# Two units of 128, 160 or 192 tokens with stationary weights, in place of an expert's last two tiles

## The chip, the core and the metric

The kernel runs on one core of one Trainium2 chip. Its time is the device time of one execution in microseconds; the time before is the median of three runs, 766.85 us (766.51 to 767.8). The core has five engines with instruction streams of their own: TensorE (PE in the profile; PEld is its loading of weights), VectorE (DVE), ScalarE (ACT), GpSimd (POOL) and SyncE (SP). Each works through its stream in order and waits on semaphores for the others. SP issues the loads of weights here, and POOL issues gathers and scatters of single rows.

## The reference, cut to what matters

The first half is block-sparse attention over 4 x 8 heads of 768 tokens. The change leaves its arithmetic alone. Its result is laid out as 3072 rows of 512 numbers, and each row goes through one of eight experts:

```python
N, D, E, F = (3072, 512, 8, 1024)
logits = x @ w_gate
expert_idx = np.argmax(logits, axis=1)
...                                   # gate_w: the softmax weight of the expert that was chosen
for e in range(E):
    lo, hi = (boundaries[e], boundaries[e + 1])
    h = np.maximum(x_sorted[lo:hi] @ w1[e], 0.0)      # layer 1: 512 -> 1024
    y_sorted[lo:hi] = h @ w2[e]                       # layer 2: 1024 -> 512
y = y_sorted[inv_perm]
return (gate_w[:, None] * y).astype(np.float32)
```

Everything is float32. How many rows an expert gets is known on the chip only, during the run. For the inputs of this case the reference gives

| | expert 0 | 1 | 2 | 3 | 4 | 5 | 6 | 7 |
|---|---|---|---|---|---|---|---|---|
| rows in all | 431 | 32 | 256 | 32 | 256 | 160 | 593 | 1312 |
| rows left after the first five tiles | 175 | 32 | 256 | 32 | 128 | 32 | 465 | 1312 |
| tiles of 128 that these need | 2 | 1 | 2 | 1 | 1 | 1 | 4 | 11 |

The first five tiles (`KA = 5`, phase A) are laid out while the last quarter of the attention still runs, from the first three quarters of the rows. The rest (phase B) is laid out once all rows are there: 23 tiles, so 28 in all.

## The kernel before: what the change touches

A tile is 128 rows of one expert. Its rows are gathered, turned so that features lie on the partitions, and taken through the two layers. In layer 1 the weights are stationary and 128 tokens move past them, in layer 2 the tokens are stationary and 512 columns of weights move.

```python
def layer1(i, *between):
    hT = st[i]["hT"] = xp.tile([P, FB, P], F32, name="hT")
    for g in range(2):
        hp = upper["ps_h"].tile([P, FB // 2, P], F32, name="hp")     # two PSUM banks in this pool
        for m in range(FB // 2):
            fb = g * (FB // 2) + m
            for c in range(DB):
                nc.tensor.matmul(hp[:, m, :], lhsT=st[i]["w1"][:, c, fb * P : (fb + 1) * P],
                                 rhs=st[i]["xT"][:, c, :], start=(c == 0), stop=(c == DB - 1))
        if g == 0 and i >= KA:
            nc.vector.tensor_relu(hT[:, : FB // 2, :], hp[:])
        else:
            nc.scalar.activation(hT[:, g * (FB // 2) : (g + 1) * (FB // 2), :], hp[:], AF.Relu)
        if g == 0:
            for do in between:
                do()

def layer2(i, group):
    zp = upper["ps_z"].tile([P, DM], F32, name="zp")
    for fb in range(FB):
        nc.tensor.matmul(zp[:], lhsT=st[i]["hT"][:, fb, :], rhs=st[i]["w2"][:, fb, :],
                         start=(fb == 0), stop=(fb == FB - 1))
    ...   # ScalarE scales by the gate weight, GpSimd scatters the 128 rows to the output
```

The loop over tiles; `fetch` loads 2 MB of weights into one of two buffers of its layer, `turn_x` turns the rows (on VectorE from the seventh tile on). Two points matter below: the layout of phase B (`layout_b`, a chain of small VectorE operations) runs beside tiles 1 and 2, and `tokens("B", ...)`, 24 small matmuls that need the last result of that chain, stands in TensorE's stream ahead of the second layer of tile 1.

```python
for i in range(NT):                       # NT = 24 tiles in any case, the rest in one arm of a switch
    if i == 0:
        ranks("B", TA, NT)
    gather(i + 3)
    if i + 1 < NT:
        layer1(i + 1, lambda: turn_x(i + 2))
        fetch(i + 3, 1)
    if i == 0:
        count("B")
        layout_b()
    if i == 1:
        tokens("B", NT, NB_)
    layer2(i, "rows_out")
    fetch(i + 2, 2)
    ...
for arm in tc.Switch(nc.values_load(rt["arm"][0:1, 0:1], min_val=0, max_val=REDO), REDO + 1):
    ...                                   # arm 4 here: tiles 24 to 27
```

The end of the chain of `layout_b`:

```python
og = [left > 128 * t for each t]; nt = sum(og); up = running sum of nt   # five operations
tile_experts("B", up, NB_)            # xeB: the expert of each tile, read by the loads of weights
...                                   # offsets of each expert's rows, the slot of each row
one_hots("B", sl, NT, NB_)            # sl -> row and tile number -> ocB, tkB, and orB in 4 pieces of 6
```

(The first line is shortened to words; the operations are in the whole kernel.)

## Time and profile before

| | |
|---|---|
| time, median of three | 766.85 us |
| span of the profiled execution | 765.7 us |
| TensorE busy | 749.5 us, 98% of the span |
| VectorE / ScalarE / GpSimd busy | 415.8 / 270.2 / 67.2 us |
| attention, first matmul of the first tile | up to about 357 us |
| tiles, from there to the last matmul | about 357 to 755 us |
| bytes moved by DMA | 157.57 MB, mean 206 GB/s; 300 to 360 GB/s in most slices of the tile stage |

How to read the profile: its second part cuts the span into 40 slices and gives each engine's busy share in tenths; its fourth part follows the chain of work that ended last back from the end, and says for each piece which engine held it; its fifth part groups instructions by the source line, with the number of instructions, the busy time, the mean duration of one, and the idle time just ahead of them with what ended it. An engine that is busy 98% of the span and holds 86% of the chain is the one whose work sets the time. Matmuls overlap, so their durations are longer than their spacing: the spacing is what counts, and it is read from the chain. A float32 matmul of the source appears as two instructions in the trace: 32 matmuls of a tile's layer 1 as 64, and 8 of layer 2 as 16.

### The profile page before, as it was taken

How to read it: one execution, taken by the hardware profiler on the slowest of the kernel's cores; microseconds unless marked ns; L12 is line 12 of the kernel's file. 1: busy time of each engine (PE TensorE's matmuls, PEld its weight loads, DVE VectorE, ACT ScalarE, POOL GpSimd, SP SyncE). 2: the span in 40 equal slices, each digit the busy share in tenths (PEclk: the TensorE clock that was granted, in tenths of full speed). 3: DMA queues.
4: the chain of work that ended last, by engine and by line, in shares of the span. 5: the costliest groups of instructions: out<-in, count | busy, mean ns of one | idle time of the engine just before them, and what ended most of it. 6: DMA issues, size and time to landing. Idle time of an engine off the chain costs nothing.

```text
span 765.7 us, 13053 instructions
## 1 busy us (share of the span) xinstructions
PE 749.5 (98%) x5134; PEld 475.8 (62%) x5134; DVE 415.8 (54%) x834; ACT 270.2 (35%) x425; POOL 67.2 (9%) x98
## 2 busy tenths in 40 slices
PE   7999999999999999999999999999999999999994
PEld 4555555555555555556777686786776776866682
DVE  4678777777778779997530235533434425323400
ACT  4666676667666675665111000100100100001000
POOL 4000000000000000002011121111111211211010
PEclk8999999999999999999999999999999999999998
DMA  8322333233322331842789989899899899899940
GB/s 187 83 60 48 82 84 85 63 83 84 85 56 51 83 84 44 319 165 78 244 308 333 344 311 348 320 329 346 320 329 362 314 344 345 320 346 339 355 147 6
DMA packets 119362, 157.57 MB, mean 206 GB/s; under 512 B 56499, under 2 KB 72947, under 8 KB 119284
## 3 DMA queue, kind: packets, MB, share of 16 engines
q1 hardware_dynamic: 112672, 142.42, 55.8%
q0 software_dynamic: 4480, 13.75, 4.6%
q8 instruction: 43, 0.70, 0.4%
q10 hardware_dynamic: 2132, 0.41, 0.3%
q14 instruction: 35, 0.29, 0.1%
HBM read 143.79 MB, written 13.73 MB: 206 GB/s over the span
## 4 chain that ended last, share of the span: by engine, by line
PE 86%; DMA 7%; issue 5%; another core or an unknown queue 0%; ACTq 0%; POOL 0%; ACT 0%; DVE 0%; POOLq 0%
PE hp L661 21%; PE zp L676 19%; PE s L216 17%; PE op L237 16%; DMA out_dram<-zo,sB 6%; PE s L219 4%; PE sp L250 3%; PE xr L270 3%; PE tp L199 2%; DMA q_sb<-in_q_dram 1%; PE tpg L650 0%; POOL xg L620 0%; ACT qT L201 0%; ACTq L117 0%
## 5 line engine op out<-in xcount | busy, mean ns | idle before, releaser
L661 PEld LDWEIGHTS hp<-xgT,w 128*128 128x128 f32 x1792 | 204.7, 192 | 12.6 <-issue 8.6
L661 PE MATMUL hp<-xgT,w 128*128 128x128 f32 x1792 | 205.6, 275 | 0.0
L676 PE MATMUL zp<-w,hT 128*128 128x512 f32 x448 | 196.9, 593 | 0.0
L642 DVE STREAM_TRANSPOSE xgT<-xg 32x128 f32<-32x128 f32 x352 | 106.5, 303 | 110.0 <-DMA xg<-x_rows,gB 94.0
L216 PE MATMUL s<-qT,kT 64*128 64x384 f32 x768 | 159.2, 493 | 0.9 <-ACT qT L201 0.9
L221 ACT ACTIVATE e<-s 128x768 f32<-128x768 f32 x192 | 152.4, 812 | 7.0 <-PE s L219 5.2
L676 PEld LDWEIGHTS zp<-w,hT 128*128 128x128 f32 x448 | 83.0, 190 | 94.2 <-issue 94.2
L227 DVE TENSOR_TENSOR esum<-esum,e 128x768 f32<-128x768 f32 x128 | 122.7, 958 | 14.6 <-ACT e L221 1.1
L237 PE MATMUL op<-e,v_sb 128*64 128x384 f32 x768 | 129.3, 486 | 0.0
L237 PEld LDWEIGHTS op<-e,v_sb 128*64 128x64 f32 x768 | 55.1, 137 | 68.8 <-issue 68.8
L216 PEld LDWEIGHTS s<-qT,kT 64*128 64x128 f32 x768 | 67.1, 190 | 38.4 <-issue 33.5
L257 DVE RECIPROCAL r<-ss 128x128 f32<-128x128 f32 x96 | 82.2, 912 | 1.3 <-ACT ss L252 1.3
L668 ACT ACTIVATE hT<-hp 128x512 f32<-128x512 f32 x33 | 19.7, 597 | 177.4 <-PE hp L661 174.4
L681 ACT ACTIVATE zo<-zp,xg 128x512 f32<-128x512 f32 x28 | 19.2, 687 | 176.7 <-PE zp L676 176.7
L666 DVE TENSOR_SCALAR hT<-hp 128x512 f32<-128x512 f32 x23 | 15.9, 692 | 101.4 <-issue 57.9
L227 DVE TENSOR_TENSOR esum<-e 128x768 f32<-128x768 f32 x32 | 30.6, 957 | 63.2 <-ACT e L221 63.2
L219 PE MATMUL s<-pen,oh 64*128 64x384 bf16 x384 | 63.2, 326 | 0.0
L242 ACT COPY oT<-op 128x384 f32<-128x384 f32 x32 | 15.3, 479 | 106.2 <-PE op L237 106.2
L682 POOL DMA_INDIRECT out_dram<-zo,sB x23 | 23.3, 1013 | 259.7 <-ACT zo L681 259.7
L219 PEld LDWEIGHTS <-oh 64*128 64x128 bf16 x384 | 18.9, 95 | 25.8 <-issue 0.9
L270 PEld LDWEIGHTS xr<-mix,oT 128*64 128x64 f32 (+1 forms) x372 | 24.0, 139 | 10.7 <-issue 10.7
L250 PE MATMUL sp<-esum,ones 128*64 128x384 f32 x128 | 27.7, 512 | 0.0
(174 smaller groups left out, 260.1 us busy)
## 6 DMA issues: line engine op xcount, KB each, us to landing
w<-in_moe_w_dram SPq DMA_DIRECT2D x56, 2048.0 KB
k_sb<-in_k_dram SPq DMA_DIRECT2D x32, 192.0 KB
v_sb<-in_v_dram SPq DMA_DIRECT2D x16, 384.0 KB
x_rows<-xb SPq DMA_DIRECT2D x16, 384.0 KB
q_sb<-in_q_dram SPq DMA_DIRECT2D x30, 192.0 KB
sums<-ss SPq DMA_DIRECT2D x32, 3.0 KB
q_sb<-in_q_dram ACTq DMA_DIRECT2D x2, 192.0 KB
xg<-x_rows,gB POOLq DMA_INDIRECT x23, 7.5
```

Of the source, the lines that this page charges most:

```text
L216: nc.tensor.matmul(s[:, hh, :CW], lhsT=kT[r, c * P : (c + 1) * P], rhs=qT[r, cols], start=True, stop=False)
L219: nc.tensor.matmul(s[:, hh, :CW], lhsT=oh[r, c, :], rhs=pen[r, cols], start=False, stop=True)
L221: nc.scalar.activation(e[:], s[:, :, :CW], AF.Exp, scale=scale)
L227: nc.vector.tensor_add(t[:], es[(n, half, 0)][:] if c == 1 else t[:], e[:])
L237: nc.tensor.matmul(op[hh * D : (hh + 1) * D, :], lhsT=v_sb[:, hh, c, :], rhs=e[:, hh, :], start=(c == 0), stop=(c == NCH - 1),)
L250: nc.tensor.matmul(sp[hh * D : (hh + 1) * D, :], lhsT=ones[:], rhs=esum[:, hh, :], start=True, stop=True)
L257: nc.vector.reciprocal(r[:, m * P : (m + 1) * P], ss[:, m * P : (m + 1) * P])
L270: nc.tensor.matmul(xr[j * M_ : (j + 1) * M_, m, :], lhsT=oT[:, m * P + j * M_ : m * P + (j + 1) * M_], rhs=mix[:, pr, :], start=True, stop ...
L642: nc.vector.transpose(xT[d, :, t], xg[t, :DM].rearrange("p (c q) -> p c q", c=DB)[:, :, d])
L661: nc.tensor.matmul(hp[:, m, :], lhsT=st[i]["w1"][:, c, fb * P : (fb + 1) * P], rhs=st[i]["xT"][:, c, :], start=(c == 0), stop=(c == DB - 1),)
L676: nc.tensor.matmul(zp[:], lhsT=st[i]["hT"][:, fb, :], rhs=st[i]["w2"][:, fb, :], start=(fb == 0), stop=(fb == FB - 1),)
L682: ins = nc.gpsimd.indirect_dma_start(out=out[:, :], out_offset=bass.IndirectOffsetOnAxis(ap=of("s", i, P), axis=0), in_=zo[:], in_offset=N ...
```

## The change: what it does and what it is for

The aim is to spare TensorE the work on rows that aren't there: a tile of 128 costs the same with 47 rows in it as with 128. A unit takes up to 192 tokens of one expert through both layers at once. Up to two experts get one, first those whose last tile has at most 64 rows and who have at least two tiles left (it takes the place of the last two tiles), then, if there are fewer than two such, any with a tile left (128 tokens, in place of one tile). In a unit the weights are stationary in both layers, so that the tokens move and their number is free: 128, 160 or 192. The output of layer 2 comes out turned and is turned back by TensorE. The kind is read from memory, and TensorE and ScalarE jump to one of three versions of the code.

With the counts above, expert 0 (175 rows left, 47 in its last tile) gets the first unit with 192 columns, and expert 7 (1312 left, 32 in its last tile) the second with 160. 23 tiles of phase B become 19, and two units; 21 tiles stand outside the last switch in place of 24, and its arm has 3 in place of 4.

```diff
+    AT = (10, 13)                       # the units stand ahead of layer 2 of tiles 10 and 13
+    KU = len(AT)
+    NS = KA - -(N - KA * P - KU * MW) // P                   # 21
+    NTB = NC - KA
+    NB_ = NTB + 2 * KU                                       # 26 -> 30 columns of the slot table
...
+    ea = mpool.tile([P, 8, NCH * P], F32, name="ea")         # the attention's e, 8 slots as before;
-        e = work.tile([P, 2, CW], F32, name="e", bufs=8)     # the units use its memory later
+        e = e_slot(n, half, c)
...
-            oT = work.tile([P, CW], F32, name="oT", bufs=4)
+            oT = work.tile([P, CW], F32, name="oT", bufs=3)
-        r = work.tile([P, CW], F32, name="r")
+        r = work.tile([P, CW], F32, name="r", bufs=1)
... # in summed(), for each of its two calls in layout_b:
+            nc.vector.tensor_tensor(ge[:], slot[:], wide(units[0]), op=ALU.is_ge)
+            nc.vector.tensor_tensor(ge[:], ge[:], wide(units[1]), op=ALU.mult)
+            nc.vector.tensor_tensor(slot[:], slot[:], ge[:], op=ALU.add)
... # in layout_b, ahead of tile_experts: 19 operations on 128 x 8
+        nc.vector.tensor_scalar_mul(last[:], nt[:], -float(P))
+        nc.vector.tensor_single_scalar(v_[:], nt[:], 2.0, op=ALU.is_ge)
+        nc.vector.scalar_tensor_tensor(u[:], in0=last[:], scalar=float(QR), in1=v_[:], op0=ALU.is_le, op1=ALU.mult)
+        nc.vector.tensor_tensor_scan(us[:], u[:], rt["zero"][:], 0.0, op0=ALU.add, op1=ALU.add)
+        ... 
+        nc.vector.tensor_sub(nt[:], nt[:], in_u[:])
... # and behind it: 8 for the units' experts and kinds (xeU), 3 for until and jump
+    def layers_u(u, width, banks):
+        for g in range(4):
+            hp = banks[g].rearrange("p (m t) -> p m t", m=2)
+            for m in range(2):
+                fb = 2 * g + m
+                for c in range(DB):
+                    nc.tensor.matmul(hp[:, m, :width], lhsT=st_u[u]["w1"][:, c, fb * P : (fb + 1) * P],
+                                     rhs=xT_u[:, c, :width], start=(c == 0), stop=(c == DB - 1))
+            nc.scalar.activation(hT_u[:, 2 * g : 2 * g + 2, :width], hp[:, :, :width], AF.Relu)
+        for d in range(DB):
+            zp = banks[d][:, :width]
+            for fb in range(FB):
+                nc.tensor.matmul(zp, lhsT=st_u[u]["w2"][:, fb, d * P : (d + 1) * P], rhs=hT_u[:, fb, :width],
+                                 start=(fb == 0), stop=(fb == FB - 1))
+            nc.scalar.copy(zT_u[:, d, :width], zp)
+        for j in range(2 if width > P else 1):
+            ...                          # 4 transposes each on TensorE, scaled by ScalarE into zo_u
... # in the loop over tiles:
+        if i + 3 in AT:
+            gather_u(AT.index(i + 3))    # two gathers of 128 rows by GpSimd
+        if i + 2 in AT:
+            turn_u()                     # 24 transposes of 32 x 128 on VectorE
+        if i in AT:
+            continue
+        if i + 1 in AT:
+            u = AT.index(i + 1)
+            ...                          # six banks: both of ps_h, both of ps_m, both of ps_z
+            layer2_pe(i, zps[0])
+            fetch_after(i, 2)
+            for more in tc.Switch(index, 3):          # on TensorE and ScalarE
+                weigh(i, zos[0], zps[0])
+                layers_u(u, P + more * QR // 2, banks)
+                layer2_pe(i + 1, banks[1])
+                weigh(i + 1, zos[1], banks[1])
+            fetch_after(("unit", u), 1)
+            fetch_after(("unit", u), 2)
+            fetch_after(i + 1, 2)
+            put(of("s", i, P), zos[0][:], "rows_out")
+            leave_u(u, "rows_out")                    # two scatters
+            put(of("s", i + 1, P), zos[1][:], "rows_out")
+            continue
         layer2(i, "rows_out")
```

With this TensorE's order around the first unit is: layer 1 of tile 10, layer 2 of tile 9, the unit, layer 2 of tile 10, layer 1 of tiles 11 and 12, layer 2 of tile 11. The two buffers of each layer's weights take turns in that order.

## The prediction

> **What bounds the kernel now.** I read the page's shares of busy time first, then the chain of work that ended last, with its pieces in order of time, then the timelines of TensorE and VectorE around 375 to 395 us, where the layout of phase B runs.

> ```profile
> PE 749.5 (98%) x5134; PEld 475.8 (62%) x5134; DVE 415.8 (54%) x834; ACT 270.2 (35%) x425; POOL 67.2 (9%) x98
> ...
> PE 86%; DMA 7%; issue 5%; another core or an unknown queue 0%; ACTq 0%; POOL 0%; ACT 0%; DVE 0%; POOLq 0%
> ```

> TensorE has no idle time to speak of, and holds the chain. The chain in order of time gives a tile's price:

> ```profile
> 425.81 7.14 PE hp L661 x64
> 432.95 6.87 PE zp L676 x16
> 439.82 7.14 PE hp L661 x64
> 446.96 6.87 PE zp L676 x16
> ```

> Each piece begins where the last one ends. A tile costs 7.14 + 6.87 = 14.01 us, as full as it may be. Per instruction that is 7.14/64 = 0.1116 us for 128 moving columns and 6.87/16 = 0.4294 us for 512. The line through both is 5.7 ns and 0.8275 ns a column.

> VectorE's timeline (start, duration) at the layout, and TensorE's at the same time:

> ```profile
> 374.39 0.17 DVE L454 COPY cnB<-lay 128x16 f32<-128x16 f32 x1 [3.83 <-PE lay L452]
> ...
> 376.98 0.17 DVE L475 CAST xeB<-xfB 1x26 int32<-1x26 f32 x1
> ...
> 383.09 3.56 DVE L564 TENSOR_TENSOR orB<-iota_r,rcB 128x768 bf16<-128x768 f32 x4
> ```
> ```profile
> 388.74 0.79 PE L593 MATMUL lay<-tkB,orB 128*128 128x52 bf16 x24
> 389.36 7.11 PE L676 MATMUL zp<-w,hT 128*128 128x512 f32 x16
> ```

> orB is done at 386.65, and TensorE comes to it at 388.74: 2.1 us of slack in a chain of 12.3 us.

> The queries on the switch and on the gathers:

> ```profile
> L761 PEldq TENSOR_LOAD <-arm x1: 487/487/487, 691.1 to 691.1; - x1
> L761 PEldq BRANCH_PREFETCH_HINT  x1: 50/50/50, 695.4 to 695.4; - x1
> ```
> ```profile
> DMA to landing us min/median/max: 7.0/7.7/8.1
> ```

> The first shows the switch of the kernel before: TensorE's sequencer reads its index at 691.1 us and is in the arm at 695.4, but its matmuls run without a gap until the arm's first at 698.76. The second is the time of a row gather in the tile stage (560 to 620 us); in the attention, with less traffic, the same gather took a median of 3.6 us.

> [...] at 691.1 all 32 loads and matmuls of a layer 2 that begins at 691.9 were handed over. [...] Here that took TensorE about 3.3 us, and ScalarE and VectorE about 6 us (their branches at 699.8 and 683.1, their arms at 706.1 and 689.1). [...] this trace shows two instructions for each float32 matmul of the source, each at 0.8275 ns a column[...]; I use its spacing. [...] in this trace one of 8 columns lasts 0.17 us and its dependent successor starts 0.20 us after it.

> **The change part by part.** The attention's order and waits are the same on TensorE, ScalarE and VectorE when I set the two programs side by side; smaller rings for oT and r and the fixed slots of e add no wait there. So I count only the tile stage.

> *Removed:* two tiles of expert 0 and two of expert 7, 4 x 14.01 = 56.04 us of TensorE.

> *Added, the units' matmuls:* 32 per layer in the source, 64 in the trace, 128 for both layers. At 192 columns 5.7 + 192 x 0.8275 = 164.6 ns, at 160 columns 138.1 ns: 21.07 and 17.68 us, 38.75 us together.

> *Added, turning the result back:* eight transposes per unit. Four took 0.44 us in this trace (361.86 to 362.30), so 0.9 us, ahead of which TensorE waits for ScalarE's last copy out of PSUM (some 0.33 us by the sizes of its other copies, and two semaphores) with half of the transposes beside it: 0.35 us. Both units: 2.5 us. ReLUs between the layers cost nothing: the last is needed by the 13th matmul of the second layer, 1.7 us or more after the first layer ends, and lasts about 0.5 us.

> *Added, the switches:* at the entry 6.9 us of layer 2 are queued, and the branch needs 3.3, in the worst case the 6 us of the others. The same at the exit, behind layer 2 of the next tile. Nothing.

> *Added, the longer layout:* VectorE's stream gains 19 operations of 8 columns ahead of xeB. By their waits 13 of them follow what they need (0.20 us or a little less), 6 don't (0.09 us, as 376.98 to 377.07 shows): 3.2 us. Eight for the units' kinds: 1.3 us. Three for until and jump: 0.4. Three of 128x144 (0.345 us from start to start) and three of 128x48 (0.245): 1.75. ocB and both tkB grow from 26 to 30 columns: 0.36. Sum 7.0 us, all ahead of orB. orB ends at 393.65 in place of 386.65; with the semaphore and the last six small matmuls (0.3 us) layer 2 of tile 1 starts at about 393.95 in place of 389.52: **4.4 us** of TensorE standing still. The loads of weights don't suffer: xeB is ready at about 380.3, and the load that comes next waits for a buffer until 381.35.

> *Added, behind each unit:* the unit takes the pool's two PSUM banks out of step. In the built program both halves of layer 1 of tile 11, and of tile 14, lie in the same bank, so the second half has to wait for VectorE's ReLU of the first. Undisturbed that is a semaphore (0.25 us), 0.69 us and another semaphore: 1.1 us. For tile 14 I take that. For tile 11 VectorE's stream has six of the second unit's transposes ahead of that ReLU, and they wait for the second unit's gather. It is issued behind two scatters of the first unit, about 26.5 us after the unit starts (22.3 us of unit, 0.7 us of scaling twice on ScalarE, 1.3 us per scatter). TensorE is through with the first half at 22.3 + 6.9 + 3.6 = 32.8. With 3.6 us of gather the rows land at 30.4 and nothing is lost beyond 1.1 us; with 7.7 us at 34.5, and then transposes (2.0), ReLU and semaphore make it 37.4, 4.6 us. Loads of weights are sparser beside a unit, so I take 2.2 us. Both: **3.3 us**.

> *Moved off the path:* two experts' weights fewer, 8.4 MB. Loads were issued when a buffer came free (SP's own waits name hp and zp for 143 and 138 us) and TensorE never waited for one, so they give nothing back. In the program after, the loads for tiles 11 and 12 are released inside the switch, by each layer of the unit.

> Sum: -56.04 + 38.75 + 2.5 + 4.4 + 3.3 = -7.1 us; 766.85 - 7.1 = 759.8 us. I predict **759.6 us**.

> **The rivals.** (1) The layout's wait is hidden, because TensorE can be behind by then, or because operations of 8 columns overlap more than I count: then 755 us. Against it: TensorE's stream is fixed there and had 2.1 us of slack only. (2) The weights pile up: during a unit of some 20 us only two loads are asked for, and behind it layers of 7 us follow each other. If the load for tile 12 were released only at the switch's end, it would come about when it is needed, and the next ones late: 3 to 6 us per unit, 766 to 770 us. Against it: it is released by the unit's own first layer, some 18 us ahead of its use. (3) The jumps aren't hidden [...]: up to 3 us at each of four branches, 765 us or more. Against it: the old switch cost nothing under the same load. (4) The gather of the second unit is as slow as in the trace's tile stage: 762 us. (5) With narrow moving tiles the loading of weights sets the pace: PEld takes 192 ns each, but at 128 columns they already follow at 111.6 ns, and at 160 and 192 there is more room.

> **Range and chances.** The gain of the units alone (14.8 us) is below 2% (15.3 us), so faster by over 2% would need all waits gone and more. Slower than 782 us would need the rivals all together. The range is set by the layout's wait (3.5 to 5.5), the waits behind the units (2.2 to 6) and jumps (0 to 3): 756.0 to 763.0. Chances: faster 0.02, within 2% 0.96, slower 0.02.

> **What would show each step.** In the profile after: 24 tiles of 14.01 us in the chain (1536 and 384 instructions of the two layers); 128 instructions of unit matmuls in about 21.1 us for the first unit and 17.7 for the second; a hole in TensorE of about 4.4 us ahead of the 24 matmuls of tokens, ended by VectorE's orB; a hole of 1 to 4.6 us inside layer 1 of tile 11 and of about 1.1 us inside that of tile 14, both ended by VectorE's ReLU; no hole at the switches' entries and exits; no wait of TensorE for weights. I am wrong if the attention's part isn't the same to a microsecond, if TensorE waits for a load of weights, or if a jump shows as a hole.

## The result and the profile after

The kernel after takes 763.04 us (median; 761.92 to 763.64), the kernel before 766.85: a ratio of 0.9947, with an interval of 0.9929 to 0.9964. The change brings 3.8 us (by the interval 2.8 to 5.4) where 7.3 were predicted; the median lies at the upper edge of the range that was given (756.0 to 763.0).

The page of the kernel after: the shares of busy time, the clock granted to TensorE in 40 slices, and the chain of work that ended last.

```profile
PE 738.1 (97%) x5086; PEld 477.4 (63%) x5086; DVE 413.3 (54%) x850; ACT 273.9 (36%) x437; POOL 67.1 (9%) x100
...
PEclk8999999999999999999999999999999999999997
...
PE 48%; issue 37%; DMA 7%; POOL 4%; DVE 2%; another core or an unknown queue 0%; ACTq 0%; POOLq 0%; ACT 0%
```

TensorE has 11.4 us less to do by its busy time (749.5 to 738.1), and the span shrinks by 5.1 (765.7 to 760.6). The chain is not the one that the prediction looked for: this time it runs from the last scatter back along GpSimd's own order ("issue" is time in which GpSimd waited for nothing that is on record), and GpSimd is busy 9% of the span. Such a chain names no bound; the idle time of TensorE does. TensorE's waits (engine and line, what ended them, us in all, times, the longest), first before and then after:

```profile
PE bm L162 <- DVE allow L155: 2.6, 1, 2.6
...
```
```profile
PE lay L658 <- DVE orB L629: 3.4, 4, 1.8
PE hp L748 <- DVE hT L753: 3.0, 2, 2.1
PE bm L175 <- DVE allow L168: 2.6, 1, 2.6
...
```

The waits left out are 1.4 us or less and the same ones in both. Two waits are new, both of those that the prediction named: the layout's and the one behind the units. None is a wait for weights. The first new wait in the timelines of the kernel after (start, duration, and in brackets the idle time before it), VectorE and then TensorE:

```profile
389.60 3.56 DVE L629 TENSOR_TENSOR orB<-iota_r,rcB 128x768 bf16<-128x768 f32 x4
```
```profile
390.61 0.34 PE L658 MATMUL lay<-tkB,orB 128*128 128x60 bf16 x6 [1.81 <-DVE orB L629]
391.52 0.34 PE L658 MATMUL lay<-tkB,orB 128*128 128x60 bf16 x6 [0.57 <-DVE orB L629]
392.35 0.34 PE L658 MATMUL lay<-tkB,orB 128*128 128x60 bf16 x6 [0.48 <-DVE orB L629]
393.22 0.34 PE L658 MATMUL lay<-tkB,orB 128*128 128x60 bf16 x6 [0.53 <-DVE orB L629]
393.40 8.81 PE L762 MATMUL zp<-w,hT 128*128 128x512 f32 x16
```

orB is done at 393.16, and layer 2 of tile 1 starts at 393.40 in place of 389.36; the tile stage began 0.1 us earlier, so that the wait is 4.13 us. (Holes below are taken in this way, from where the next instruction would have started at full pace. The bracket counts from the modelled end of the one before and is up to 0.2 us less.) But look at the last line: the same 16 instructions took 7.03 us elsewhere, here 8.81. The granted clock goes with it. This view cuts the time into stretches: busy time of each engine (with the number of instructions), then the granted clock, the DMA engines' share and GB/s.

```profile
390.60:394.20 3.60, 2.01 (x26) 1.33 (x27) 3.09 (x7) 0.00 (x0) 0.00 (x0) 1.00 0.99 348
394.20:397.60 3.40, 3.40 (x5) 1.35 (x4) 2.63 (x9) 0.00 (x0) 1.90 (x2) 0.50 0.92 325
397.60:401.00 3.40, 3.40 (x9) 1.52 (x8) 1.21 (x5) 0.00 (x0) 0.00 (x0) 1.00 0.28 88
...
547.80:551.20 3.40, 1.26 (x12) 1.13 (x11) 3.24 (x11) 0.00 (x0) 0.00 (x0) 1.00 1.03 388
551.20:554.60 3.40, 3.40 (x19) 3.40 (x18) 3.28 (x13) 0.00 (x0) 0.00 (x0) 0.50 0.70 262
554.60:558.00 3.40, 3.40 (x32) 3.40 (x32) 2.94 (x11) 0.60 (x1) 0.00 (x0) 1.00 0.39 80
```

From 394.2 to 397.6 us TensorE is busy all the time at half its clock: 5 matmul instructions in 3.4 us, 9 in the next 3.4. The same once more at 551.2 to 554.6, inside tile 11, where VectorE and TensorE show:

```profile
547.55 1.89 DVE L806 STREAM_TRANSPOSE ea<-ea 32x128 f32<-32x128 f32 x6 [30.67 <-DMA ea<-x_rows,gB]
549.38 0.64 DVE L753 TENSOR_SCALAR hT<-hp 128x512 f32<-128x512 f32 x1
```
```profile
544.20 3.73 PE L748 MATMUL hp<-xgT,w 128*128 128x128 f32 x32
550.07 12.61 PE L748 MATMUL hp<-xgT,w 128*128 128x128 f32 x96 [2.14 <-DVE hT L753]
...
613.27 10.98 PE L748 MATMUL hp<-xgT,w 128*128 128x128 f32 x96 [0.84 <-DVE hT L753]
```

The first half of tile 11's layer 1 is over at 547.8. The second needs the same PSUM bank, so it waits for the ReLU, and the ReLU stands behind six transposes of the second unit's rows, which had been asked for at 541.30 and could start at 547.55. The hole is 2.3 us. In tile 14 (the last line) there are no such transposes; the hole is 1.0 us (612.27 to 613.27), with the ReLU in it from 612.53 to 613.22, and the clock stays at 1.00. The 96 matmul instructions behind the hole take 12.61 us in tile 11 and 10.98 in tile 14: 1.6 us more where the clock was at half.

Where the first unit begins and where the layer behind it begins:

```profile
515.46 5.36 PE L817 MATMUL hpu<-ea,w 128*128 128x192 f32 x32
...
537.33 7.03 PE L762 MATMUL hpu<-w,hT 128*128 128x512 f32 x16
```

The bill of the kernel after, in us of TensorE, against the prediction's terms:

| term | predicted | measured | from |
|---|---|---|---|
| four tiles removed | -56.04 | -56.04 | 1536 instructions of layer 1 stand in the trace: 24 tiles; four at the 14.01 us of the kernel before |
| the two units, turning back included | +41.25 | +40.30 | 515.46 to 537.33 and 583.40 to 601.83 |
| wait for the layout | +4.4 | +4.13 | above |
| waits behind the units | +3.3 | +3.3 | 2.3 and 1.0 |
| switches | 0 | 0 | no gap at 515.46 and 583.40 |
| half clock behind two of the holes | none | +3.4 | 2 stretches of 3.4 us at half with TensorE busy throughout, each 1.7 |
| sum | -7.1 | -4.9 | |

The two profiled executions took 767.37 and 762.45 us: 4.9 less. The medians differ by 3.8; single executions scatter (761.92, 762.45, 763.62 and 763.64 for the kernel after), and 4.9 lies inside the interval. So of the 3.5 us that are missing against 7.3 the bill explains 2.2; what sets the rest, the scatter, stays open.

### The profile page after: what moved, and what is told of

It reads as the page before. It is cut to its first block, busy times and chain, and to the rows that moved or that the text cites. A ratio compares the mean times of both kernels' runs of the same rounds, so it can differ in the third digit from the quotient of the medians.

```text
span 760.6 us, 12979 instructions
## 1 busy us (share of the span) xinstructions
PE 738.1 (97%) x5086; PEld 477.4 (63%) x5086; DVE 413.3 (54%) x850; ACT 273.9 (36%) x437; POOL 67.1 (9%) x100
## 4 chain that ended last, share of the span: by engine, by line
PE 48%; issue 37%; DMA 7%; POOL 4%; DVE 2%; another core or an unknown queue 0%; ACTq 0%; POOLq 0%; ACT 0%
PE s L229 17%; PE op L250 16%; DMA out_dram<-zo,sB 7%; PE s L232 4%; PE sp L263 3%; PE xr L283 3%; PE tp L212 2%; POOL xg L686 2%; PE hp L748 2%; POOL out_dram L777 1%; DMA q_sb<-in_q_dram 1%; POOL ea L796 1%; DVE orB L629 0%; DVE tkB L649 0%
## 5 line engine op out<-in xcount | busy, mean ns | idle before, releaser
L748 PEld LDWEIGHTS hp<-xgT,w 128*128 128x128 f32 x1536 | 176.9, 193 | 13.1 <-issue 7.9
L748 PE MATMUL hp<-xgT,w 128*128 128x128 f32 x1536 | 178.2, 277 | 3.0 <-DVE hT L753 3.0
L762 PE MATMUL zp<-w,hT 128*128 128x512 f32 x352 | 156.4, 598 | 0.0
L234 ACT ACTIVATE ea<-s 128x768 f32<-128x768 f32 x192 | 152.4, 812 | 6.7 <-PE s L232 4.9
L240 DVE TENSOR_TENSOR esum<-esum,ea 128x768 f32<-128x768 f32 x128 | 122.6, 958 | 14.4 <-ACT ea L234 0.9
L250 PE MATMUL op<-ea,v_sb 128*64 128x384 f32 x768 | 129.3, 486 | 0.0
L729 DVE STREAM_TRANSPOSE xgT<-xg 32x128 f32<-32x128 f32 x288 | 87.2, 303 | 69.5 <-DMA xg<-x_rows,gB 51.8
L762 PEld LDWEIGHTS zp<-w,hT 128*128 128x128 f32 x352 | 65.9, 192 | 75.2 <-issue 75.2
L250 PEld LDWEIGHTS op<-ea,v_sb 128*64 128x64 f32 x768 | 55.1, 137 | 68.8 <-issue 68.8
L240 DVE TENSOR_TENSOR esum<-ea 128x768 f32<-128x768 f32 x32 | 30.6, 957 | 63.3 <-ACT ea L234 63.3
L255 ACT COPY oT<-op 128x384 f32<-128x384 f32 x32 | 15.3, 479 | 105.2 <-PE op L250 105.2
```

The source lines that it names most:

```text
L234: nc.scalar.activation(e, s[:, :, :CW], AF.Exp, scale=scale)
L240: nc.vector.tensor_add(t[:], es[(n, half, 0)] if c == 1 else t[:], e)
L250: nc.tensor.matmul(op[hh * D : (hh + 1) * D, :], lhsT=v_sb[:, hh, c, :], rhs=e[:, hh, :], start=(c == 0), stop=(c == NCH - 1),)
L729: nc.vector.transpose(xT[d, :, t], xg[t, :DM].rearrange("p (c q) -> p c q", c=DB)[:, :, d])
```

## The experiments

Theory A: every term of the prediction held, and what is missing is TensorE's clock, which goes to half behind a hole that is long enough. A hole then costs its length and some 1.7 us. Theory B: a hole costs its length alone, and the missing us lie elsewhere. Theory C: a hole that is taken away comes back as another wait (weights, jumps), so that little is won.

| run | what it is | us | ratio to the kernel before [interval] |
|---|---|---|---|
| e1_tokens_later | after, tokens one layer later | 757.34 | 0.9868 [0.9851, 0.9884] |
| e2_banks | after, PSUM banks kept in step | 757.92 | 0.987 [0.9854, 0.9887] |
| e3_both | both | 753.38 | 0.9813 [0.9797, 0.983] |
| e4_dose35 | before, 35 operations in the layout | 773.6 | 1.0084 [1.0067, 1.0101] |
| e5_dose18 | before, 18 operations | 767.99 | 1.001 [1.0001, 1.0019] |
| e9_dose70 | before, 70 operations | 782.0 | 1.019 [1.0173, 1.0207] |
| e7_no_switch | after, no jump tables | 763.37 | 0.9949 [0.9929, 0.9968] |
| e8_both_no_switch | e3_both, no jump tables | 757.41 | 0.9868 [0.985, 0.9887] |
| e10_turn_later | e8, second unit's transposes later | 750.75 | 0.979 [0.9777, 0.9803] |
| e11_index_early | e3_both, indices read earlier | 750.88 | 0.9793 [0.978, 0.9807] |
| e12_both_again | e3_both once more | 752.31 | 0.9814 [0.98, 0.9827] |

The ratio is to the kernel before as it was timed beside each group: 767.15 us for e1 to e4, 767.43 for e5 and e7 to e9, 766.62 for e10 to e12.

### Taking the holes away

The layout's hole goes if TensorE has a layer of 7 us to do while VectorE makes orB:

```diff
-        if i == 1:
-            tokens("B", NT, NB_)
...
         layer2(i, "rows_out")
+        if i == 1:
+            tokens("B", NT, NB_)
         fetch_after(i, 2)
```

> The changed kernel with the 24 small matmuls of the layout moved behind layer 2 of tile 1, so that TensorE doesn't stand still for orB. Theory A (a hole costs its length, and behind a long one TensorE's clock is granted at half for 3.4 us, which costs 1.7 us more): 763.0 - 4.1 - 1.7 = 757.2 us, and no stretch at half clock around 395 us. Rival B (a hole costs its length alone, the lower clock is chance): 758.9 us. Rival C (the wait only moves to the gathers and loads behind the layout): 762 to 763 us.

757.34 us, where A had 757.2. TensorE's timeline around the place:

```profile
388.28 7.03 PE L762 MATMUL zp<-w,hT 128*128 128x512 f32 x16
395.15 0.85 PE L658 MATMUL lay<-tkB,orB 128*128 128x60 bf16 x24
395.83 3.82 PE L748 MATMUL hp<-xgT,w 128*128 128x128 f32 x32
```

No hole, layer 2 at its 7.03 us, and no half clock there. The profiled executions took 762.45 (the kernel after) and 758.03 us: 4.4 less. In this run a new hole of 1.8 us stands at the first unit's entry, of which more below. The wait's 4.13 and the clock's 1.75 less this 1.8 make 4.1; without the clock, as B has it, it would be 2.3. That the median meets A's number is in part luck, since A didn't have the new hole.

Tile 11's and tile 14's holes go if the unit leaves the two banks of ps_h in step, so that the halves of layer 1 alternate again:

```diff
-            zr = banks[(4, 0)[j]]
+            zr = banks[(2, 3)[j]]
...
-                layer2_pe(i + 1, banks[1])
-                weigh(i + 1, zos[1], banks[1])
+                layer2_pe(i + 1, banks[4])
+                weigh(i + 1, zos[1], banks[4])
```

> The changed kernel with the units' last transposes and layer 2 of the tile beside each unit in other PSUM banks, so that the two halves of layer 1 of tiles 11 and 14 lie in two banks again. Theory A: the holes of 2.3 and 1.0 us go, and so does the half clock behind the longer one: 763.0 - 3.3 - 1.7 = 758.0 us. Rival B: 759.7 us. Rival C (TensorE waits for VectorE's ReLU or transposes a little later): 762 to 763 us.

757.92 us, A's number, and layer 1 of tile 11, with that of tile 12 behind it, is one piece:

```profile
544.88 14.45 PE L748 MATMUL hp<-xgT,w 128*128 128x128 f32 x128
```

The hole in tile 14, which had no transposes ahead of its ReLU, went with the bank alone. For tile 11 the run leaves open which of the two it was: in its built program the scheduler, which orders each engine's instructions when the program is built, has also moved the transposes behind that ReLU. (A run below shows that transposes alone can do it.) The profiled execution took 758.27 us, 4.2 less than that of the kernel after and not 5.0, because the layout's hole had two stretches of 3.41 us at half clock this time (391.4 to 398.2): layer 2 of tile 1 lasted 9.33 us in place of 8.81. Both edits together:

> Both edits. Theory A: 757.2 - 5.0 = 752.2 us, TensorE without a hole from the first tile to the last and its clock never at half. Rival B: 755.6 us. Rival C: 760 us or more.

753.38 us, 9.7 less than the kernel after (8.8 between the profiled executions), where the lengths of the holes make 7.4 (4.13 + 2.3 + 1.0), and a new hole of 1.25 us stands at the first unit's entry. B had 755.6 without such a hole; A had 752.2, and that hole is of the size that it lacks. C holds in part: something does come back at the unit's entry, but 1.25 to 1.8 us, not the whole gain.

### Making a hole in the kernel before

If A is right, a hole must bring the half clock without any unit. The kernel before gets operations of 128x8 that do nothing, each needing the one before it, in front of its layout's list of experts:

```diff
         nc.vector.reduce_sum(nt[:], og[:], axis=AX)
+        for _ in range(35):
+            nc.vector.tensor_scalar(nt[:], nt[:], scalar1=1.0, scalar2=None, op0=ALU.mult)
```

> The kernel before (no units) with 35 more dependent operations of 8 columns on VectorE in the layout's chain, 7.0 us: the longer layout alone. Theory A: a hole of 4.9 us less what the chain's first pieces give, about 4.5, and half clock behind it, 1.7: 766.85 + 6.2 = 773.0 us. Rival B: 771.3 us. If the layout's wait is not on the path: 766.9 us.

773.6 us, and TensorE's timeline has both parts:

```profile
390.99 0.44 PE L595 MATMUL lay<-tkB,orB 128*128 128x52 bf16 x6 [2.58 <-DVE orB L566]
...
393.60 0.44 PE L595 MATMUL lay<-tkB,orB 128*128 128x52 bf16 x6 [0.43 <-DVE orB L566]
393.86 8.79 PE L678 MATMUL zp<-w,hT 128*128 128x512 f32 x16
```

The tile stage began 0.5 us earlier than in the kernel before (357.00 against 357.49), so layer 2's start at 393.86 is 5.0 us late, and it lasts 1.76 us longer: 6.75 us in all from the first tile on. The medians differ by 6.45 (773.6 against 767.15).

Half the dose (18 in place of 35), to see whether a short hole does it too:

> The kernel before, with 18 extra dependent VectorE operations of 128x8 in the layout (18 x 0.205 = 3.7 us; 2.1 us of it are slack, so TensorE stands about 1.6 us, in pieces). Theory A (a hole of some 2 us brings half clock for about 3.4 us behind it, a shorter one doesn't): no drop, TensorE's mean clock as before, 766.9 + 1.6 = 768.5 us. Theory A' (every hole, also a short one, is followed by the drop): 770.2 us. Theory B (a hole costs its own length and the time is proportional): 768.5 as well, and it is the granted clock behind the hole that tells A and B apart from A'.

767.99 us, and the clock is 1.00 in every slice from 386 to 400 us: no drop. TensorE's idle pieces were 0.49 and 0.54 us by the brackets, and layer 2 of tile 1 starts 1.4 us late. By the medians the run costs 0.6 us (767.43 beside it; by the interval 0.1 to 1.5), where A and B had 1.6, so the time doesn't show the length exactly; the clock shows that a short hole brings no drop, as in tile 14. And a long one, with 70 operations of 128x18 on the slots, behind the list of experts:

```diff
         summed(sl[:, TA:], "B", off)
+        for _ in range(70):
+            nc.vector.tensor_scalar(sl[:], sl[:], scalar1=1.0, scalar2=None, op0=ALU.mult)
         one_hots("B", sl, NT, NB_)
```

> The kernel before, with 70 extra dependent VectorE operations of 128x18 in the layout, behind the list of experts, so that the weights' loads are asked for as before (70 x 0.205 = 14.3 us; less 2.1 of slack: TensorE stands about 12.2 us). Theory A (the drop of the clock is an event that costs a fixed 1.7 to 1.9 us per hole): 766.9 + 12.2 + 1.8 = 780.9 us. Theory A2 (what the clock loses grows with the hole's length, 1.9 us for the 4.5 us of the run with 35 operations, so 5.2 here): 784.3 us. Theory B (no cost besides the hole): 779.1 us.

782.0 us, which is neither number of A's: more than a fixed 1.8, less than in proportion; B's 779.1 is missed as well. TensorE's timeline and the clock, each stretch in one line as above:

```profile
398.60 0.44 PE L595 MATMUL lay<-tkB,orB 128*128 128x52 bf16 x6 [10.42 <-DVE orB L566]
...
401.47 9.60 PE L678 MATMUL zp<-w,hT 128*128 128x512 f32 x16
```
```profile
389.20:392.80 3.60, 0.00 (x0) 0.00 (x0) 3.01 (x18) 0.00 (x0) 0.00 (x0) 1.00 0.77 289
392.80:406.40 13.60, 6.51 (x30) 3.35 (x31) 11.05 (x31) 0.00 (x0) 0.00 (x0) 0.50 0.26 95
406.40:410.00 3.60, 3.60 (x9) 1.52 (x8) 0.00 (x0) 0.00 (x0) 0.00 (x0) 0.99 0.00 0
```

The clock is at half for 13.65 us, but for the first 8.6 of them TensorE had hardly anything to do. Only what lies beside layer 2, 401.5 to 406.5, costs: 9.60 - 7.03 = 2.6 us. Layer 2 starts 12.8 us late against the first tile, which itself began 0.7 us earlier than in the kernel before (356.78 against 357.49): 12.8 + 2.6 - 0.7 = 14.7, and the medians differ by 14.6 (782.0 against 767.43).

This gives theory A its form: the cost is half of the work that lies in the half-clock stretches (2.6 of 5.0 us here). These stretches at half clock last 3.42 and 3.41 us in the kernel after, 6.83 with 35 operations, 13.65 with 70: one, two and four times 3.41 (13.65 / 4 = 3.41). From the end of the first in the kernel after (397.6) to the start of the second (551.2) it is 153.6 us, 45 times 3.413. Holes of 2.2 us (e1, in tile 11) and 2.3 us brought the drop.

If the time is cut at the edges of those stretches and on from there in steps of 3.413 us, TensorE was busy in the step ahead of a drop for 0.37 and 0.54 of it in the kernel after, 0.41 in the runs with tokens moved, with banks in step and with 35 operations. Steps that were busy for 0.47 to 0.82 were followed by full clock, among them the one around the jump's hole of 1.8 us (0.52). The two kinds overlap. These shares use modelled ends, above all the 0.54, which has the layout's small matmuls in it. If a matmul counts only for its spacing (5.7 ns + 0.8275 ns a column for float32; some 28 ns for the layout's of 60 columns, 24 of which take 0.68 us in e1, from 395.15 to 395.83), the steps ahead of a drop come to some 0.36 or less and the others to 0.42 or more, in all the traces here. So, as an estimate from these shares, the border lies near 0.4 of a step, and whether a hole of some 2 us crosses it can depend on where it lies between two edges. In the kernel after an edge at 390.78 cuts the layout's hole into steps of 0.47 and 0.54, and half clock began behind the second, at 394.20; in e2_banks the step in which the hole begins had 0.41 (387.98 to 391.39), and half clock began at 391.39. To come back took more: at half clock, steps busy for 0.46 (e4), 0.49 (e8), 0.68 (e2), 0.73 (e7) and 0.75 (e9) were each followed by another at half.

### The jumps

The holes at the first unit's entry in e1 and e3 were the prediction's third rival, in runs other than the one that it was about. First the kernel after with the widths written in, valid for this input's counts only:

```diff
-            index = {ET.PE: nc.tensor.value_load(at, ...), ET.Activation: nc.scalar.value_load(at, ...)}
-            for more in tc.Switch(index, 3):
-                layers_u(u, P + more * QR // 2, banks)
-                ...
+            layers_u(u, P + (2, 1)[u] * QR // 2, banks)
+            ...
```

> The kernel after without its jump tables: the widths are written in (192 for the first unit, 160 for the second), which is what the counts of this input choose. Theory A (in the kernel after both jumps lie behind the 6.9 us of queued layer 2): 763.0 us, no difference. Rival (the jumps cost 1.3 to 1.8 us each, also where the trace shows no hole): 760 to 761 us.

763.37 us: no difference in time, as A had it, but it isn't the same kernel without a jump. In the build without the switch all 24 transposes of the second unit stand ahead of tile 11's ReLU, where the kernel after has six there. The two halves of layer 1 of tile 11, and of tile 14, follow each other without a gap, so the banks seem to be in step here without the edit of e2. Behind the units TensorE waits once, for 3.5 us ahead of tile 12's layer 1, with two stretches of 3.41 us at half clock (553.3 to 560.1), and not at all in tile 14. That much else changed, so this run doesn't tell what a jump costs; that it costs nothing in the kernel after rests on its timeline, where the unit follows layer 2 without a gap. The same edit on the run with both repairs:

> The run with tokens moved and the banks kept in step, and the jump tables left out, the widths written in. Theory A (the hole of 1.25 us at the first unit's entry in that run is the jump, which took 6.1 us where layer 2 covers 6.9 less the reading of its index): the hole goes, 753.4 - 1.25 = 752.1 us, and no more than 0.3 us of hole at either unit's entry. Rival (the hole is the unit's own: its transposes or its first weights are late): 753.4 us, hole as before.

757.41 us, 4 us slower, which no theory had. TensorE's timeline shows two things:

```profile
502.61 7.03 PE L762 MATMUL zp<-w,hT 128*128 128x512 f32 x16
509.48 5.36 PE L817 MATMUL hpu<-ea,w 128*128 128x192 f32 x32
...
549.28 9.83 PE L748 MATMUL hp<-xgT,w 128*128 128x128 f32 x64 [3.94 <-DVE hT L753]
```

The hole at the unit's entry is gone, so it was the jump's. In its place stands one of 4.1 us (3.94 in the bracket) ahead of tile 12's layer 1, which needs the bank that tile 11's ReLU has to free, with half clock from 547.6 to 554.4: here the banks are in step, and the transposes, all 24 ahead of that ReLU, are enough. If the transposes are held back behind the next tile's ReLU,

```diff
+        if i + 2 == AT[1]:
+            with tc.issue_after(st[i + 1]["relu"].ins):
+                turn_u()
```

> The run without jump tables (tokens moved, banks in step), with the 24 transposes of the second unit's rows issued on VectorE behind tile 12's first ReLU and no longer ahead of tile 11's. Theory A (that run was slow because those transposes kept the ReLU waiting: a hole of 3.9 us, and half clock behind it): both go, 757.4 - 3.9 - 1.7 = 751.8 us, mean clock 0.994. Rival (the hole moves to another tile, or the clock's share isn't there): 753.5 us or more.

it is 750.75 us, and TensorE has no wait left in the tile stage. That is 1.0 us less than A had: A counted one stretch of 3.41 us at half clock, but 5.1 us of work lay at half behind that hole (549.3 to 554.4), which took 9.83 us in place of 7.31. The last question is whether the jump can stay. The group of branch instructions of e3_both on TensorE's sequencer (duration least/median/greatest in ns, first and last start), and that of the kernel after:

```profile
L1018 PEldq COMPARE_BRANCH  x4: 317/2176/6142, 505.2 to 594.4; - x4
```
```profile
L1018 PEldq COMPARE_BRANCH  x4: 328/2586/5144, 508.7 to 601.6; - x4
```

In the kernel after the branch starts at 508.7, with layer 2 (508.59), and is through after 5.14 us, before layer 2 ends at 515.46. In e3_both it starts at 505.2, 1.7 us behind the start of layer 2 (503.49), takes 6.14 us, and layer 2 ends at 510.4. The reason for the late start is the order of TensorE's stream: in the kernel after both indices are read between the layout's matmuls (390.6 us); moving the tokens pushed both reads to the switch, 1.9 us of sequencer time (503.3 to 505.2) behind layer 2. So they are moved back ahead of it:

```diff
+            if u == 0:
+                indexes = [{ET.PE: nc.tensor.value_load(...), ET.Activation: nc.scalar.value_load(...)} for j in range(KU)]
+            index = indexes[u]
             layer2_pe(i, zps[0])
```

> The run with tokens moved and banks in step, jump tables as in the kernel after, with both units' indices read by TensorE and ScalarE ahead of tile 9's layer 2 and not behind it. In that run TensorE's sequencer began to read them at 503.3 us, was at the branch at 505.2 and through it at 511.4; layer 2 was over at 510.4. Theory A (the hole of 1.25 us is the end of the jump): the branch starts some 1.5 us earlier and ends about 509.8, the hole goes, 753.4 - 1.25 = 752.2 us. Rival ([...] it varies by more than the 1.5 us): a hole stays, 753 us or more.

> The run with tokens moved and banks in step once more, on the chip of the two kernels beside it, so that they are compared with it there. Every theory expects 753.4 us, within 0.15%; the hole at the first unit's entry (1.25 us before) is the jump's by theory A and may differ by a microsecond from run to run, by the rival it is the same.

750.88 against 752.31 us on the same chip, 1.4 us where A had 1.25. TensorE's timeline of the first:

```profile
502.82 7.03 PE L762 MATMUL zp<-w,hT 128*128 128x512 f32 x16
509.69 5.37 PE L817 MATMUL hpu<-ea,w 128*128 128x192 f32 x32
```

No hole; the branch started at 502.9 and took 3.9 us. In e12 it started at 504.6 and took 5.85 us:

```profile
510.71 5.44 PE L817 MATMUL hpu<-ea,w 128*128 128x192 f32 x32 [0.79 <-DVE xgT L729]
```

That is a hole of 0.95 us, with another of 0.4 at the second unit's entry. All five executions of e11 (750.63 to 751.5) lie below all five of e12 (751.98 to 753.57). The bracket names VectorE's transposes of the next rows (xgT), but the unit doesn't wait for them: in e11 it starts at 509.69, and the same transposes last until 511.41. How much of e11's gain is the earlier start of the branch and how much its shorter duration wasn't separated. How long the branch took varied from 3.3 us (the last switch of the kernel before, 692.0 to 695.3) to 6.6 (e1); why it varied stays open. This version keeps the jumps and does all that the kernel after does. It is 15.7 us faster than the kernel before (766.62 on that chip; by the interval 14.8 to 16.9), and by the bill above that is what the units save: 56.04 - 40.30 = 15.7 (that the two agree to 0.1 us is luck, given the interval).

## Why the prediction was right or wrong

- **The tiles removed and the units.** Right; the spacing of 5.7 ns + 0.8275 ns a column held within 2% for 160 and 192 columns. 20.80 us of matmuls in the first unit (21.07 predicted) and 17.39 in the second (17.68), 1.07 and 1.04 of turning back (1.25 each). Rival 5, weight loading, didn't show.
- **The longer layout.** Right: orB ended at 393.16 (393.65 predicted), the wait was 4.13 us. The prediction's 4.4 counts from 389.52, while the line that it shows has layer 2 start at 389.36; from there its own working gives 4.6. Rival 1 fell.
- **Behind each unit.** Right in both numbers, 2.3 and 1.0 us (2.2 and 1.1), though the 2.2 was picked between 1.1 and 4.6. The cause is shown for tile 14 (the shared bank, with 0.26 us ahead of the ReLU, 0.69 of ReLU and 0.05 behind it); for tile 11, bank and transposes together, how much each had of it wasn't separated. Rival 4's slow gather came in part: rows asked for at 541.3 could be turned at 547.55, 6.25 us later, between the 3.6 and the 7.7 that the prediction had. (Its sum for when they are asked for, 22.3 + 2 x 0.7 + 2 x 1.3, is 26.3 us behind the unit's start, and its 30.4 and 34.5 assume 26.8; measured were 25.8.)
- **The step that failed** is the price of the holes in "Added, the longer layout" and "Added, behind each unit": 4.4 us "of TensorE standing still" and 3.3 us were entered in the sum as their lengths and nothing else. The two longer ones each had 3.41 us at half clock behind them, 1.7 us each; the run with 35 operations shows the same cost without a unit, and the two repairs gave it back. With it the prediction's own sum, -7.1, would have been -3.7 (its 759.6 also stands 0.2 below that sum); the profiled bill is -4.9, because the units and the layout's wait cost 1.2 less than predicted. That the median still reached the edge of the range is luck: the range left room for slower waits and for jumps, and the clock used it up. The clock had no term and no rival, though the profile's row of the clock and the mean clock (0.992 before, 0.986 after) are where it shows. A caution on that mean: it counts half-clock stretches at the start of the execution and behind TensorE's last matmul too (8.8 to 15.7 us and from 759.8 us on in the kernel before), so it must be read by stage.
- **The switches.** Right for this kernel, for the reason given: the jump (508.7 to 513.8 us) lies beside layer 2's queued matmuls, which run until 515.46. But the figure of 3.3 us was too small: 5.1 us here and up to 6.6 elsewhere, near or above its worst case of 6. It fitted because both indices had long been read. Rival 3 was real, and one repair brought it out.
- **The weights.** Right; TensorE waits for none, also at 750.75 us. Rival 2 fell.
- **The chain** as a test was wrong: it took GpSimd's way and shows no 24 tiles. The counts of instructions and the timeline served in its place.

## What to carry to other kernels

Price a hole in a full TensorE stream by its length and by half of whatever work lies in the half-clock stretch behind it. Here holes of up to 1.8 us brought no drop of the clock and holes of 2.2 us and more did, at 1.7 us for a drop of 3.41 us; by the estimate above it is TensorE's busy share of such a step that counts, so a hole of that size can fall on either side. When an edit inserts work into a rotation of two buffers, check which buffer the next user gets: one step out of phase made a pipelined pair wait for itself. And when code is moved past a jump or a jump is taken out, look at what the scheduler moves with it: the reading of an index and a set of transposes each cost more than a microsecond here.
